# Products of w3 and w_out ahead of block 4's convolution, which moves between second products; w2's first casts on POOL

## The chip, the core and the metric

The kernel runs on one core of one Trainium2 chip. A core has five engines with an instruction queue each: PE (matrix products), DVE and ACT (element-wise work, the only two that take results out of PSUM here), POOL (element-wise work in SBUF, and a queue that issues DMAs) and SP (a queue that only issues DMAs). Sixteen DMA engines move the data of all queues. The metric is the device time of one execution in microseconds (us); less is better.

## What is computed

A light-weight convolution along the sequence, then a multiplicative feed-forward part without any non-linearity:

```python
def _attn_ref(x, weight):                 # x (8, 3904, 192), weight (8, 7)
    w = softmax(weight, axis=-1)          # in the reference written out
    x_pad = zeros(6 rows) + x             # along the sequence
    out[b, s, h, :] = sum_k w[h, k] * x_pad[b, s + k, h, :]   # 8 heads of 24 columns
def _moe_ref(x, w1, w2, w3, w_out):       # x (31232, 192), d_ff 1024
    a = x @ w1
    b = x @ w2
    h = a * b @ w3
    return h @ w_out                      # (31232, 192) fp32
```

Since nothing non-linear stands between w3 and w_out, the kernel forms W = w3 @ w_out once (1024 x 192) and computes (a * b) @ W.

## The kernel before, in words

The 31232 tokens are two halves of 15616 (index r = 0, 1), which lie on partitions 0 to 63 and 64 to 127. Along a half, tokens are cut twice. For the convolution they are *windows* of 58 tokens (64 rows with the 6 of overlap), and windows are grouped in *blocks* (SIZES: 10, 8, 10, 8, then six of 36, then 20). For the products they are *rounds* of 512 tokens, 31 in all, handled in groups of 4.

- `conv(b, h0, nh, evict)` (L273) convolves nh heads of block b: PE multiplies the window's rows (`xb`) with a band matrix (`Aband`), into a pair of PSUM banks (there are four pairs, taken in turn); the engines in `evict` copy the result to `convo` (L290).
- `store(b)` writes `convo` to a DRAM buffer `rows` from SP's queue (L311, L317). `transposes(R)` reads `rows` back, transposed, into `xT` (L346), three DMAs for a round, also on SP's queue. `send(last)` issues the transposes of all rounds that are stored. The blocks 0 to 3 don't go this way: PE transposes them itself (`pe_transpose`, L326).
- `first_product(R)` makes a and b of a round for eight column tiles (L373); ACT copies a to SBUF (L379), and DVE multiplies it with b (L380) into `abT`.
- `second_product(R, r)` multiplies `abT` with `W_sb` (L399); ACT copies the result (L404), and a DMA writes it to the output (L411), in the first group of rounds from POOL's queue, later from SP's.
- `w3_product(jt)` makes an eighth of W (L435) from `w3T` and `wo_b`; ACT copies it to `W_sb` (L437).

`load_w3` casts w3 to bf16 into DRAM by two DMAs of POOL's queue (L425) and reads it back transposed by 16 DMAs of SP's queue (L428); the order is first columns 0 to 511 of all eight row tiles, then 512 to 1023. A tiny copy on POOL (`pace`, L472) waits for one of these transposes and so holds back what stands behind it on POOL's queue: the loads of blocks 4 and 5 (L112). The weights w1 and w2 are needed on both halves of the partitions. Their first quarter of columns comes in fp32 (`wfirst`) and is cast four times (`cast_w(i, r)`, L447), the other quarters come through casting DMAs (L162) and are copied to the upper half (L352).

The order on each queue is that of the program, since the schedule is written out by hand. It runs: weights of the convolution (`warm` keeps PE busy meanwhile, L190); block 0; first_product(0) to (3) with blocks 1 to 3 between their tiles; then block 4's convolution in three slots, heads 0 to 2, 3 to 5, 6 and 7, with three, three and two of the w3 products behind them; then for each group of rounds the first products (from group 1 on), and eight second products with the next block's convolution in the same three slots behind the second, fourth and sixth of them. A block's `store` is called behind its last slot.

Of the kernel before, what the change touches and what calls it, by code (L numbers as in the profile page):

```python
# [16 lines left out]
def kernel(  # L17
# [10 lines left out]
    nc = tc.nc  # L28
# [4 lines left out]
    DFF = moe_w1.shape[1]  # L33
    JT = DFF // 128
# [6 lines left out]
    GROUP = 4  # L41
    RING = GROUP * CH
    Q = 64
# [7 lines left out]
    NB = len(SIZES)  # L51
# [4 lines left out]
    def tok(i):  # L56
        return (i // WB) * S + (i % WB) * ST
# [29 lines left out]
    def halves_of(b):  # L87
        n = SIZES[b] // 2
        return [(FIRST[b], 2 * n)] if 2 * n <= MAXN else [(FIRST[b], n), (FIRST[b] + n, n)]
# [8 lines left out]
    def load_x(b, parts=(0, 1)):  # L98
        tiles = xb_of.setdefault(b, [])
        zeros_of = zero_rows.setdefault(b, [])  # L100
        for i0, n in [v for e, v in enumerate(halves_of(b)) if e in parts]:
            xb = work.tile([128, n, D], BF16, tag="xb", bufs=5, name="xb")
            w = 0
            while w < n:
                i = i0 + w
                m = min(n - w, WB - i % WB)
                at_end = i + m == NWIN
                if at_end:
                    m -= 1
                if m:  # L110
                    for r in range(NS):
                        nc.gpsimd.dma_start(out=xb[Q * r:Q * r + Q, w:w + m, :],  # L112
                                            in_=x_spans(r, i, m))
                if i % WB == 0:
                    zeros_of += [(xb, 0, w), (xb, 1, w)]
                w += m
                if at_end:
                    nc.gpsimd.memset(xb[Q:128, w, :], 0.0)
                    t = tok(NWIN - 1) - PAD
                    nc.gpsimd.dma_start(out=xb[0:Q, w, :], in_=x_rows[t:t + Q, :])  # L120
                    nc.gpsimd.dma_start(out=xb[Q:Q + PAD + LAST, w, :],
                                        in_=x_rows[TS + t:TS + t + PAD + LAST, :])
                    w += 1
            if len(halves_of(b)) == 1:
                tiles += [(xb, 0), (xb, SIZES[b] // 2)]
            else:
                tiles.append((xb, 0))
# [7 lines left out]
    wfirst = work.tile([Q, 2, NP, DFF // 4], FP32, tag="abT", bufs=GROUP, name="wfirst")  # L135
    pace = const.tile([1, 2], BF16)
# [15 lines left out]
    WC = (0, DFF // 4, DFF // 2, DFF * 3 // 4, DFF)  # L152
    wd = [const.tile([128, NP, DFF], BF16, name=f"wd{i}", tag=f"wd{i}") for i in range(2)]
# [5 lines left out]
    def load_w(part):  # L159
        cs = slice(WC[part], WC[part + 1])  # L160
        for i in range(2):
            nc.gpsimd.dma_start(out=wd[i][0:Q, :, cs], in_=w_rows[i][:, :, cs])  # L162
# [5 lines left out]
    for p0 in (0, Q):  # L168
        nc.gpsimd.affine_select(
            out=diag[p0:p0 + Q], in_=ones[p0:p0 + Q].to_broadcast([Q, Q + PAD]),  # L170
# [3 lines left out]
    for r in range(NS):  # L174
        nc.gpsimd.dma_start(out=xb0[Q * r + PAD:Q * r + Q, 0, :],
                            in_=x_rows[r * TS:r * TS + ST, :])
    load_w(1)
    load_w(2)
    load_x(1)
    load_w(3)  # L180
    load_x(2)
# [3 lines left out]
    def warm(n, t=None):  # L185
        p = None
        if t is None:
            p, t = banks()
        for j in range(n):
            nc.tensor.matmul(t[:, j % 2, :], zeros[:, 0:128], zeros, start=True, stop=True)  # L190
        if p is not None:
            drained(p)

    warm(4)

    wmax = const.tile([1, H], FP32)
    wsum = const.tile([1, H], FP32)
# [4 lines left out]
        out=wall, in0=wall, in1=wmax.unsqueeze(2).to_broadcast([1, H, K]), op=ALU.subtract)  # L202
# [6 lines left out]
        out=wrow, in0=wall, in1=wsum.unsqueeze(2).to_broadcast([1, H, K]), op=ALU.mult)  # L209
# [20 lines left out]
    def band(g, e, f):  # L230
        c = slot([128, K, Q], BF16, "cprod")
        nc.vector.tensor_tensor(
            out=c, in0=taps, in1=wsb[:, g, e].unsqueeze(2).to_broadcast([128, K, Q]),
            op=ALU.mult)
        p, bps = banks()
        for v, lhsT in enumerate((ident, swapped)):
            for k in range(K):
                nc.tensor.matmul(bps[:, 0, v * Q:v * Q + Q], lhsT, c[:, k, :],
                                 start=(k == 0), stop=(k == K - 1))
        f(out=Aband[:, g, e].rearrange("p v s -> p (v s)"), in_=bps[:, 0, 0:2 * Q])  # L240
        drained(p)
# [15 lines left out]
    def conv(b, h0, nh, evict=None):  # L257
        n = SIZES[b] // 2
        if h0 == 0:
            convo_of[b] = work.tile([128, n, NP, NS, Q], BF16, tag="convo", bufs=2, name="convo")  # L260
        convo = convo_of[b]
        p, cps = banks()
        wd = nh * G

        def view(ps, r):
            return cps[ps, r, 0:n * wd].rearrange("p (w g) -> p w g", g=wd)

        for j in range(nh):
            h = h0 + j
            for c in range(2):  # L270
                xb, w0 = xb_of[b][c]
                for r in range(NS):
                    nc.tensor.matmul(  # L273
                        view(slice(Q * c, Q * c + Q), r)[:, :, j * G:(j + 1) * G],
                        band_of(h, r),
                        xb[Q * r:Q * r + Q, w0:w0 + n, h * G:(h + 1) * G],
                        start=True, stop=True)
        src = cps[:, :, 0:n * wd].rearrange("p r (w g) -> p r w g", g=wd)
        o, moves = 0, []
        for k, c0, m in segments(h0 * G, wd):  # L280
            moves.append((convo[:, :, k, :, c0:c0 + m].rearrange("p w r g -> p r w g"),
                          src[:, :, :, o:o + m]))
            o += m
        if h0 + nh == H:
            del xb_of[b]
        if evict == ():
            return p, moves
        for e, (dst, part) in enumerate(moves):
            f = evict or [nc.scalar.copy]
            f[e % len(f)](out=dst, in_=part)  # L290
        drained(p)
# [128 lines left out]
    w3T = const.tile([128, JT, DFF], BF16)  # L420
# [11 lines left out]
    def w3_product(jt):  # L432
        p, wps = banks()
        for gt in range(JT):
            nc.tensor.matmul(wps[:, 0, 0:D], w3T[:, gt, jt * 128:(jt + 1) * 128],  # L435
                             wo_b[:, gt, :], start=(gt == 0), stop=(gt == JT - 1))
        nc.scalar.copy(out=W_sb[:, jt, :], in_=wps[:, 0, 0:D])  # L437
        drained(p)


    V, A, P = nc.vector.tensor_copy, nc.scalar.copy, nc.gpsimd.tensor_copy
# [1 line left out]
    def move(f, pair):  # L443
        f(out=pair[0], in_=pair[1])  # L444

    def cast_w(i, r, f):
        f(out=wd[i][Q * r:Q * r + Q, :, 0:WC[1]], in_=wfirst[:, i])  # L447

    cast_w(0, 0, A)
    band(0, 0, A)  # L450
    band(0, 1, A)
    band(1, 0, A)
    band(1, 1, V)
    cast_w(0, 1, A)
    cast_w(1, 1, V)
    cast_w(1, 0, A)
    warm(1)
    for h, f in ((0, V), (2, A), (4, V), (6, A)):
        p, moves = conv(0, h, 2, ())
# [9 lines left out]
            copy_w(part, i, f)  # L469
    load_w3()  # L470
    nc.gpsimd.dma_start(out=wo_b, in_=wor)
    P(out=pace, in_=w3T[0:1, JT // 2 - 1, DFF - 2:DFF])  # L472
    load_x(4)
    load_x(5)

# [6 lines left out]
    def send(last):  # L482
        while sent[0] <= min(last, NR - 1) and min((sent[0] + 1) * CH, TS) <= stored[0]:
            transposes(sent[0])
            sent[0] += 1
# [13 lines left out]
    def zero(b):  # L499
        for xb, r, w in zero_rows.pop(b, []):  # L500
            nc.gpsimd.memset(xb[Q * r:Q * r + PAD, w, :], 0.0)  # L501

    def conv_heads(b, heads):
        for h in heads:
            conv(b, h, 1, (V,))
        if heads[-1] == H - 1:
            store(b)

    slots = (range(0, 3), range(3, 6), range(6, H))
    zero(4)  # L510
    for i, heads in enumerate(slots):
        conv_heads(4, heads)
        for jt in range(3 * i, min(3 * i + 3, JT)):
            w3_product(jt)

    groups = [list(range(R, min(R + GROUP, NR))) for R in range(0, NR, GROUP)]
    assert groups[-1][-1] == NR - 1
    for p, rounds in enumerate(groups):
        b = PROLOGUE_BLOCKS + p
        order = rounds[-1:] + rounds[:-1] if rounds[-1] == NR - 1 else rounds  # L520
        for j, R in enumerate(order if p else ()):
            first_product(R)
            send(R + GROUP)
            if j < 2 and b < NB:
                P(out=pace, in_=abT_of[R][0:1, JT - 1, 1, 0:2])  # L525
                load_x(b, (j,))
        if b < NB:
            zero(b)
        if p == 0:
            send(2 * GROUP - 1)  # L530
        for i, (R, r) in enumerate((R, r) for R in rounds for r in range(NS)):
            second_product(R, r, R == NR - 1 and r == 1, nc.sync if p else nc.gpsimd)
            if i in (1, 3, 5) and b < NB:
                conv_heads(b, slots[i // 2])
    assert sent[0] == NR


# [28 lines left out]
```

## Time and profile before

| | us |
|---|---|
| median of 3 runs | 526.74 (526.51 to 527.09) |
| the profiled execution | 528.84 |
| its span | 527.1 |
| PE busy | 515.7 |
| DVE busy | 362.4 |
| ACT busy | 323.0 |
| POOL busy | 53.9 |

The profile is of one execution. PE, DVE, ACT and POOL are listed with their instructions; SPq is SP's queue of DMA issues, whose lengths are the time of issuing and not of the transfer. "out<-in" names the tiles, "x64" counts merged instructions, and brackets give the idle time of the engine ahead of them with what ended it. The granted PE clock of the core is 1.00.

### The profile page before, as it was taken

The numbers are of one execution on the slowest core, as the hardware profiler recorded it, in microseconds if no ns is written. First come the engines' busy times: TensorE is split into PE (matmuls) and PEld (weight loads), VectorE is DVE, ScalarE is ACT, GpSimd is POOL, SyncE is SP. The second block draws the span as 40 slices with busy tenths as digits, with TensorE's granted clock in tenths as the row PEclk, the third lists the DMA queues.
The fourth block names the chain that finished last, engine by engine and source line by source line (L and its number), as shares of the span: only waits on it lengthen the run. The fifth ranks groups of instructions, "written<-read, shape, count | busy, mean of one in ns | idle before, by whom it ended". The sixth has DMA issues, their size and how long they took to land.

```text
span 527.1 us, 12790 instructions
## 1 busy us (share of the span) xinstructions
PE 515.7 (98%) x5463; PEld 344.6 (65%) x5463; DVE 362.4 (69%) x351; ACT 323.0 (61%) x409; POOL 53.9 (10%) x91
## 2 busy tenths in 40 slices
PE   7999799999999999999999999999999999999997
PEld 4555479655796557955579555895558945599567
DVE  6777855599655996569964699637994289921880
ACT  5888532677526775367743677437774377744762
POOL 8304102112000110001200020000300000000000
PEclk9999999999999999999999999999999999999999
DMA  9997999999648882478834798357643632024004
GB/s 134 229 119 102 180 139 215 191 174 137 111 136 191 113 118 72 140 181 118 111 91 131 170 119 109 91 145 170 90 67 95 169 93 41 17 91 150 2 1 150
DMA packets 133381, 64.59 MB, mean 123 GB/s; under 512 B 90234, under 2 KB 132620, under 8 KB 133260
## 3 DMA queue, kind: packets, MB, share of 16 engines
q1 hardware_dynamic: 94378, 44.10, 38.4%
q0 software_dynamic: 38800, 19.58, 29.6%
q8 instruction: 42, 0.69, 0.6%
q14 instruction: 15, 0.12, 0.1%
q10 hardware_dynamic: 146, 0.10, 0.1%
HBM read 33.25 MB, written 36.52 MB: 132 GB/s over the span
## 4 chain that ended last, share of the span: by engine, by line
PE 85%; DMA 7%; SPq 3%; POOL 2%; DVE 1%; issue 1%; ACT 0%; POOLq 0%; ACTq 0%; DVEq 0%
PE pairs L373 52%; PE pairs L399 30%; DMA xb<-in_x_dram 3%; SPq L428 3%; PE pairs L273 2%; DMA w3rows<-in_moe_w_dram 2%; DMA xT<-rows 1%; POOL xb L112 1%; DVE convo L290 1%; DMA w3T<-w3rows 1%; POOL wd L352 1%; PE pairs L435 0%; POOL wd L162 0%; POOL xb L165 0%; DVE abT L380 0%
## 5 line engine op out<-in xcount | busy, mean ns | idle before, releaser
L380 DVE TENSOR_TENSOR abT<-asb,pairs 128x1024 bf16<-128x1024 bf16 (+1 forms) x248 | 298.5, 1204 | 79.8 <-ACT asb L379 42.6
L373 PE MATMUL pairs<-xT,wd 64*128 64x512 bf16 (+1 forms) x2976 | 320.2, 373 | 1.6 <-DMA xT<-rows 0.6
L379 ACT CAST asb<-pairs 128x1024 bf16<-128x1024 f32 (+1 forms) x248 | 247.6, 998 | 69.2 <-PE pairs L373 68.6
L373 PEld LDWEIGHTS <-wd 64*128 64x128 bf16 x2976 | 165.4, 94 | 150.5 <-issue 3.8
L399 PE MATMUL pairs<-W_sb,abT 128*128 128x192 bf16 x1952 | 165.6, 246 | 0.0
L399 PEld LDWEIGHTS <-abT 128*128 128x128 bf16 x1952 | 159.8, 98 | 8.7 <-issue 8.7
L404 ACT COPY osb<-pairs 128x384 f32<-128x384 f32 x122 | 58.2, 477 | 116.7 <-PE pairs L399 116.7
L290 DVE CAST convo<-pairs 128x864 bf16<-128x864 f32 (+5 forms) x70 | 53.7, 825 | 66.6 <-PE pairs L273 61.3
L112 POOL DMA_DIRECT2D xb<-in_x_dram x40 | 31.0, 791 | 10.1 <-PE pairs L373 6.2
L525 POOL COPY pace<-abT 1x2 bf16<-1x2 bf16 x10 | 1.7, 174 | 241.4 <-DVE abT L380 241.4
L273 PE MATMUL pairs<-xb,Aband 64*64 64x432 bf16 (+3 forms) x352 | 17.4, 294 | 3.3 <-POOL xb L501 2.7
L273 PEld LDWEIGHTS <-Aband 64*64 64x64 bf16 x352 | 7.1, 105 | 10.9 <-issue 9.7
L411 POOL DMA_DIRECT2D out_dram<-osb x8 | 6.1, 758 | 27.8 <-ACT osb L404 27.8
L437 ACT CAST W_sb<-pairs 128x192 bf16<-128x192 f32 x8 | 2.5, 318 | 9.8 <-PE pairs L435 9.8
L404 DVE COPY osb<-pairs 128x192 f32<-128x192 f32 x1 | 0.4, 357 | 11.1 <-PE pairs L399 11.1
L435 PE MATMUL pairs<-wo_b,w3T 128*128 128x192 bf16 x64 | 6.4, 246 | 0.3
L435 PEld LDWEIGHTS <-w3T 128*128 128x128 bf16 x64 | 5.2, 97 | 2.0 <-issue 2.0
L290 ACT CAST convo<-pairs 128x512 bf16<-128x512 f32 (+3 forms) x12 | 5.5, 508 | 0.0
L326 PE MATMUL pairs<-identw,convo 128*128 128x128 bf16 x54 | 4.2, 219 | 1.0 <-DVE convo L444 0.9
L326 PEld LDWEIGHTS <-convo 128*128 128x128 bf16 x54 | 3.2, 97 | 2.8 <-issue 1.5
L190 PE MATMUL pairs<-zeros 128*128 128x512 bf16 x7 | 3.4, 602 | 1.3 <-DVE zeros L145 1.3
L162 POOL DMA_DIRECT2D wd<-in_moe_w_dram x6 | 3.8, 640 | 0.0
(51 smaller groups left out, 39.8 us busy)
## 6 DMA issues: line engine op xcount, KB each, us to landing
out_dram<-osb SPq DMA_DIRECT2D x52, 384.0 KB
xb<-in_x_dram POOLq DMA_DIRECT2D x18, 432.0 KB, 8.4
rows<-convo SPq DMA_DIRECT2D x9, 648.0 KB
out_dram<-osb POOLq DMA_DIRECT2D x8, 384.0 KB, 6.0
w3rows<-in_moe_w_dram POOLq DMA_DIRECT2D x2, 1024.0 KB, 12.4
xb<-in_x_dram POOLq DMA_DIRECT2D x6, 240.0 KB, 7.1
xT<-rows SPq DMA_TRANSPOSE x81
rows<-convo SPq DMA_DIRECT2D x9, 135.0 KB
```

Source lines behind the costliest of these rows:

```text
L112: nc.gpsimd.dma_start(out=xb[Q * r:Q * r + Q, w:w + m, :], in_=x_spans(r, i, m))
L273: nc.tensor.matmul(view(slice(Q * c, Q * c + Q), r)[:, :, j * G:(j + 1) * G], band_of(h, r), xb[Q * r:Q * r + Q, w0:w0 + n, h * G:(h + 1) ...
L290: f[e % len(f)](out=dst, in_=part)
L326: nc.tensor.transpose(out=tps[:, w, :], in_=convo[:, w, k].rearrange("p r g -> p (r g)"), identity=ident)
L373: nc.tensor.matmul(p[:, r, 0:N], wd[i][rs, k, ft * 128:(ft + 1) * 128], xT[k][rs, r0:r0 + N], start=(k == 0), stop=(k == NP - 1))
L379: nc.scalar.copy(out=asb[:, :, 0:N], in_=pa[:, :, 0:N])
L380: nc.vector.tensor_tensor(out=ab[:, ft, :, 0:N], in0=asb[:, :, 0:N], in1=pb[:, :, 0:N], op=ALU.mult)
L399: nc.tensor.matmul(ops[:, (g - g0) * D:(g - g0) * D + D], ab[:, jt, r, g * 128:(g + 1) * 128], W_sb[:, jt, :], start=(jt == 0), stop=(jt = ...
L404: f(out=osb[:, g0:g0 + per, :].rearrange("p g d -> p (g d)"), in_=ops[:, 0:per * D])
L411: queue.dma_start(out=out[t0:t0 + ng * 128, :].rearrange("(g p) d -> p g d", p=128), in_=osb)
L428: nc.sync.dma_start_transpose(out=w3T[:, gt, j:j + CH], in_=w3rows[j:j + CH, gt * 128:(gt + 1) * 128])
L435: nc.tensor.matmul(wps[:, 0, 0:D], w3T[:, gt, jt * 128:(jt + 1) * 128], wo_b[:, gt, :], start=(gt == 0), stop=(gt == JT - 1))
```

## The change

The eight w3 products stand directly behind first_product(3). Heads 0 to 2 of block 4 follow them; heads 3 to 5 stand behind the first second product, heads 6 and 7 (with the store) behind the second. Block 4's evictions alternate between DVE and ACT, head by head. In the first group of rounds block 5's slots stand behind the fourth, sixth and seventh second product in place of the second, fourth and sixth, and the transposes of rounds 4 to 7 are issued behind block 4's store as before. Both first casts of w2 are done by POOL, behind the loads of the second and third quarter of w1 and w2 and ahead of block 1's loads; those of w1 both by ACT, ahead of the bands. One more warm matmul runs at the start. `pace` waits for the transpose of row tile 1 of w3's second half of columns in place of that of row tile 3.

```diff
+    def cast_w(i, r, f):
+        f(out=wd[i][Q * r:Q * r + Q, :, 0:WC[1]], in_=wfirst[:, i])
+
     load_w(1)
     load_w(2)
+    cast_w(1, 0, nc.gpsimd.tensor_copy)
+    cast_w(1, 1, nc.gpsimd.tensor_copy)
     load_x(1)
     load_w(3)
     load_x(2)
...
-    warm(4)
+    warm(5)
...
     cast_w(0, 0, A)
+    cast_w(0, 1, A)
     band(0, 0, A)
     band(0, 1, A)
     band(1, 0, A)
     band(1, 1, V)
-    cast_w(0, 1, A)
-    cast_w(1, 1, V)
-    cast_w(1, 0, A)
     warm(1)
...
-    P(out=pace, in_=w3T[0:1, JT // 2 - 1, DFF - 2:DFF])
+    P(out=pace, in_=w3T[0:1, 1, DFF - 2:DFF])
...
-    def conv_heads(b, heads):
-        for h in heads:
-            conv(b, h, 1, (V,))
+    def conv_heads(b, heads, f=(nc.vector.tensor_copy,)):
+        for j, h in enumerate(heads):
+            conv(b, h, 1, (f[j % len(f)],))
         if heads[-1] == H - 1:
             store(b)
 
     slots = (range(0, 3), range(3, 6), range(6, H))
     zero(4)
-    for i, heads in enumerate(slots):
-        conv_heads(4, heads)
-        for jt in range(3 * i, min(3 * i + 3, JT)):
-            w3_product(jt)
+    for jt in range(JT):
+        w3_product(jt)
+    conv_heads(4, slots[0], (V, A))
...
         if b < NB:
             zero(b)
+        at = {1: [(b, slots[0])], 3: [(b, slots[1])], 5: [(b, slots[2])]}
         if p == 0:
-            send(2 * GROUP - 1)
+            at = {0: [(4, slots[1], (V, A))], 1: [(4, slots[2], (V, A))],
+                  3: at[1], 5: at[3], 6: at[5]}
         for i, (R, r) in enumerate((R, r) for R in rounds for r in range(NS)):
             second_product(R, r, R == NR - 1 and r == 1, nc.sync if p else nc.gpsimd)
-            if i in (1, 3, 5) and b < NB:
-                conv_heads(b, slots[i // 2])
+            for c in at.get(i, ()) if b < NB else ():
+                conv_heads(*c)
+            if p == 0 and i == 1:
+                send(2 * GROUP - 1)
```

More of the change, by code (lines that the diff above doesn't have):

```diff
@@ L444, in move @@
         f(out=pair[0], in_=pair[1])
-    def cast_w(i, r, f):
-        f(out=wd[i][Q * r:Q * r + Q, :, 0:WC[1]], in_=wfirst[:, i])
     cast_w(0, 0, A)
+    cast_w(0, 1, A)
     band(0, 0, A)
```

## The prediction

> **What bounds the kernel now.** I read the page's busy times first, then the chain of waits, then the timelines of PE, DVE, SP and POOL between 44 and 114 us and of all engines in the first 18 us. Columns of the chain: start, length, what; of the timelines: start, length, engine, line, operation, and in brackets the idle time before and who ended it.
>
> ```profile
> span 527.1 us, 12790 instructions
> PE 515.7 (98%) x5463; PEld 344.6 (65%) x5463; DVE 362.4 (69%) x351; ACT 323.0 (61%) x409; POOL 53.9 (10%) x91
> ```
>
> PE is busy for 98%, so only its idle times can be won, some 11 us. The chain shows the largest below 100 us.
>
> ```profile
> 71.55 1.43 PE pairs L435 x16
> ...
> 78.26 0.67 PE pairs L273 x12
> ...
> 90.93 6.44 DMA xT<-rows
> ...
> 97.41 41.18 PE pairs L373 x380
> 138.59 5.39 PE pairs L399 x64
> ```
>
> From 97.41 on PE runs from product to product with no wait on the chain: whatever the change does ahead of that moment, the end moves by as much as the start of first_product(4) moves. That start is set by a DMA, xT<-rows, and not by PE. PE's own list shows how close the two were:
>
> ```profile
> 47.34 13.28 PE L373 MATMUL pairs<-xT,wd 64*128 64x512 bf16 x120
> ...
> 63.44 0.34 PE L273 MATMUL pairs<-xb,Aband 64*64 64x432 bf16 x1 [2.52 <-POOL xb L501]
> 63.98 0.70 PE L273 MATMUL pairs<-xb,Aband 64*64 64x432 bf16 x9 [0.20 <-POOL xb L501]
> ...
> 67.46 0.74 PE L273 MATMUL pairs<-xb,Aband 64*64 64x432 bf16 x12 [0.21 <-DVE convo L290]
> ...
> 70.99 0.56 PE L273 MATMUL pairs<-xb,Aband 64*64 64x432 bf16 x8 [0.21 <-DVE convo L290]
> ...
> 96.18 0.60 PE L373 MATMUL pairs<-xT,wd 64*128 64x512 bf16 x4
> 97.41 2.96 PE L373 MATMUL pairs<-xT,wd 64*128 64x512 bf16 x25 [0.62 <-DMA xT<-rows]
> ```
>
> first_product(3) ends at 47.34+13.28=60.62. Then PE idles 2.52+0.20+0.21+0.21=3.14 us inside block 4's convolution, arrives at first_product(4) at 96.18 and waits 0.62 us there. The chain behind xT is this:
>
> ```profile
> 71.42 2.02 DVE L290 CAST convo<-pairs 128x864 bf16<-128x864 f32 x2 [0.48 <-PE pairs L273]
> 73.47 0.34 SPq L317 DMA_DIRECT2D rows<-convo  x1
> ...
> 79.68 2.48 SPq L311 DMA_DIRECT2D rows<-convo  x1
> 82.20 4.17 SPq L317 DMA_DIRECT2D rows<-convo  x2
> 86.55 1.88 SPq L346 DMA_TRANSPOSE xT<-rows  x1
> ```
>
> The last eviction of block 4 ends at 71.42+2.02=73.44; SP then issues the seven copies of store(4) until 86.37 and the transposes of round 4 from 86.55; the third, issued at 90.93, lands at 97.37. From eviction to xT: 97.37-73.44=23.93 us. This chain starts at the **end of the convolution of block 4**, and that is the point the change moves.
>
> **The change part by part.** *Products first.* The 64 matmuls of w3 x w_out now follow first_product(3) at once: 16 took 1.43 us, so 0.089 each and 5.7 us (bounds 5.4, what 64 of L399 take, and 6.8, the stretches they needed among the convolutions). Then come conv heads 0 to 2 (0.67), second_product(0,0) (half of 5.39: 2.69), heads 3 to 5 (0.67), second_product(0,1) (2.69), heads 6 and 7 (0.56): 12.98 us together. Nothing here waits for block 4's loads, which land at 63.09 (below). The eviction of the last head is by ACT; its price isn't in the trace at this size, so I take DVE's 2.02/2=1.0 us.
>
> *The first casts.* In the beginning:
>
> ```profile
> 7.62 1.69 ACT L447 CAST wd<-wfirst 64x768 bf16<-64x768 f32 x2
> ...
> 8.40 0.95 DVE L447 CAST wd<-wfirst 64x768 bf16<-64x768 f32 x1
> 9.38 1.29 DVE L444 CAST convo<-pairs 128x480 bf16<-128x480 f32 x3
> ...
> 8.43 0.82 PE L273 MATMUL pairs<-xb,Aband 64*64 64x120 bf16 x32
> 10.19 1.12 PE L326 MATMUL pairs<-identw,convo 128*128 128x128 bf16 x15 [0.94 <-DVE convo L444]
> ...
> 3.75 0.21 PE L215 MATMUL pairs<-wrow,half 1*128 1x28 bf16 x2 [0.53 <-DVE wrow L208]
> ```
>
> PE's convolution of block 0 begins at 8.43, but DVE evicts from 9.38 only, behind its cast, and ACT is busy with two casts until 7.62+1.69=9.31. Without them both can start near 8.7, as the first heads are done: for DVE 0.65 earlier. I take 0.6 us off the transposes and the start of first_product(0) (at most the 0.94 idle). One w1 cast stays on ACT, moved ahead of the bands; it delays the first band's eviction by some 0.2 us, with three other banks open to PE. The fifth warm matmul lies in the 0.53 us for which PE waits for wrow.
>
> POOL takes both w2 casts between load_w(2) and load_x(1):
>
> ```profile
> 8.31 0.68 POOL L112 DMA_DIRECT2D xb<-in_x_dram  x1 [0.36 <-DMA xb<-in_x_dram]
> ...
> 13.11 3.12 POOL L352 COPY wd<-wd 64x768 bf16<-64x768 bf16 x4
> ...
> 16.83 0.36 PE L273 MATMUL pairs<-xb,Aband 64*64 64x96 bf16 x16
> xb<-in_x_dram POOLq DMA_DIRECT2D x1, 192.0 KB, 5.2
> ```
>
> A POOL copy of this size from bf16 takes 0.78; from fp32 no row exists, so 0.78 to twice that, and I take the lower, nearest row: 1.6 us (to 3.1) for two. Everything behind them on POOL's queue is later by that: both load_x(1), load_w(3), load_x(2) and (3), POOL's copies of parts 2 and 3, both w3 loads, wo_b. Block 1's second load (8.31+5.2=13.5, the last row being its time to landing) comes at 15.1, while conv(1) is due at 16.83-0.6=16.2: covered, by 1.1 us. At the upper price it is late by 0.4 us; POOL's first copy for part 2 (13.11+0.78+3.1=17.0) is late by about as much. So the prologue gives 0.6 us, between 0.95 gained and 0.5 lost.
>
> *The pace.* It waits for the tenth transpose of w3T in place of the twelfth.
>
> ```profile
> 39.85 1.26 SPq L428 DMA_TRANSPOSE w3T<-w3rows  x1
> ...
> 42.46 4.10 DMA w3T<-w3rows
> ...
> 49.98 13.11 DMA xb<-in_x_dram
> ```
>
> That is 42.46-39.85=2.6 us earlier, less the 1.6 us by which w3 is late: block 4's loads start about 1 us earlier (2.6 earlier to 0.5 later). They landed at 49.98+13.11=63.09 and are first needed at 65.7 now: this edit is worth nothing where it stands, hidden by the products.
>
> *The sum.* first_product(3) ends at 60.62-0.6=60.0; plus 12.98 gives 73.0; plus 1.0 the last eviction, **74.0 against 73.44**. PE itself goes on with second_product(1,0) to (3,1) and block 5's convolution, 5.39+0.67+5.39+0.67+2.69+0.56+2.69=18.1, and reaches first_product(4) at 91.0, 5.2 us earlier than its 96.18. It finds no xT. What the chain from eviction to xT takes then decides.
>
> ```profile
> 105.34 6.34 SPq L317 DMA_DIRECT2D rows<-convo  x4
> 113.32 2.06 SPq L346 DMA_TRANSPOSE xT<-rows  x1
> 76.44 0.79 POOL L411 DMA_DIRECT2D out_dram<-osb  x1 [12.51 <-ACT osb L404]
> ...
> 85.12 0.75 POOL L411 DMA_DIRECT2D out_dram<-osb  x1 [1.89 <-ACT osb L404]
> ...
> 94.42 0.75 POOL L411 DMA_DIRECT2D out_dram<-osb  x1 [2.48 <-ACT osb L404]
> ```
>
> Block 5, with as many rows and no output copies beside it, goes from store to first transpose in 113.32-105.34=8.0 us; block 4 needed 86.55-73.47=13.1 us with four output copies (76.44 to 85.12) beside it: some 1.3 us for each. Output copies come 0.8 us behind their second product (the first ended at 71.55+1.43+2.69=75.67, its copy is issued at 76.44), now at 69.8, 73.2, 76.5, 79.2, 82.5, 85.2, 88.6 and 91.8. Six lie where there were six; the one at 73.2 is new beside the start of the store (+1.3), and those of 94.42 and later are gone from the end of the transposes (up to -1.3). I take 23.93 unchanged, between 1.3 less and 1.3 more. [...]
>
> first_product(4) goes on at 74.0+23.93=97.9 in place of 97.4: **+0.5 us**. The profiled execution took 528.84 (span 527.1) and would take 529.3; on the median of 526.74 that is **527.2**. All 5.2 us that PE wins turn into idle time between 91.0 and 97.9.
>
> **The rivals.** *PE comes back slow* (the other side). Idle for 6.9 us, with two pairs of matmuls in between as parts of xT land, PE may lose its pace:
>
> ```profile
> 1.33 1.89 PE L190 MATMUL pairs<-zeros 128*128 128x512 bf16 x4 [1.33 <-DVE zeros L145]
> ...
> 3.89 1.03 PE L190 MATMUL pairs<-zeros 128*128 128x512 bf16 x2
> ...
> 7.86 0.46 PE L190 MATMUL pairs<-zeros 128*128 128x512 bf16 x1
> ```
>
> After the launch, four 512-column matmuls come 0.43 us apart ((1.89-1.03)/2, four against two); in first_product the two row halves run side by side, 13.28/60=0.22 per 512 columns: half pace. Slow lasted at least until 4.92 and at most until about 8 us, 3.6 to 6.7 us from the first matmul, each losing half: 1.8 to 3.3 us. The 2.52 us gap at 63.44 cost nothing (0.34 us for its next matmul), so it decides from a gap above that. Start at 97.9, then +2.5: 526.74+0.5+2.5=**529.7**. Against it: the matmuls in between cut the gap into pieces near 2.5 us. [...]
>
> *The chain shortens.* If the missing late output copies matter more than the new early one, the third transpose lands as w3T's did, 4.10 us from issue in place of 6.44: -2.3+0.5=-1.8, **524.9**. For it: output copies end 5 us earlier. Against: the store in front is no less crowded.
>
> *The change does what it says in full.* xT is there when PE arrives at 91.0: 6.4 us less, **520.3**. It needs a chain of 17 us where even uncrowded parts make 8.0+2.5+4.1=14.6 (store, two issues of 1.26, a landing); with six output copies beside it hardly.
>
> *POOL's casts cost* their upper price and the prologue loses 0.5 where I have a gain of 0.6: +1.1, **528.3**.
>
> **How the numbers follow.** Forecast 0.40; slow PE 0.28; shorter chain 0.20; POOL 0.08; in full 0.04. 0.2% of 526.7 is 1.05 us, about what a measurement of this kernel tells from nothing. The forecast (its terms spread by some 1.1 us about +0.5) gives 0.03 faster, 0.25 same, 0.12 slower; slow PE 0.01 same, 0.27 slower; shorter chain 0.15 faster, 0.05 same; POOL 0.02 same, 0.06 slower; in full 0.04 faster. Sum: faster 0.22, same 0.33, slower 0.45. The likeliest case alone runs from 526.0 to 528.6; with the rivals, leaving a tenth at each end, 524.7 to 530.0.
>
> **What would show it.** The w3 products in one piece of 5.7 us from about 60.0 with no idle; transposes of block 0 from about 9.6; first output copy near 69.8; SP's first copy of store(4) near 74.0 and its first transpose near 87; PE idle, released by xT<-rows, from 91 to about 98. Slow PE shows as L373 matmuls near 1.03-0.43=0.60 us each behind 98 us and ACT waiting twice as long for them. Wrong I am if PE meets a landed xT, if store(4) starts below 73 us, or if PE waits for xb or wd before 25 us.

## The result and the profile after

| | before | after |
|---|---|---|
| first comparison, median | 526.62 us (526.34 to 527.09, 4 runs) | 530.83 us (530.22 to 531.34, 4 runs) |
| its ratio | | 1.0079, 95% interval 1.0061 to 1.0096 |
| second comparison (e1), median | 526.96 us (34 runs) | 529.92 us (11 runs) |
| its ratio | | 1.0045, 95% interval 1.0027 to 1.0064 |
| span of the profiled execution | 527.1 | 528.3 |

By the ratios the changed kernel is slower, by 2.4 us (1.4 to 3.4) in the larger comparison and by 4.2 us in the first (0.6% to 1.0%); the medians of the larger one lie 3.0 us apart. Most of the difference between the two comparisons lies in the executions that they caught, as the mean granted PE clock of each run shows. In e1's comparison the kernel before has 23 runs at 0.999 or 1.000 (median 526.54), ten at 0.996 or 0.997 (528.53) and one at 0.994 (530.51); the changed kernel has three at 0.997 (528.89) and eight at 0.992 or 0.993 (530.08). In the first comparison all four runs of the changed kernel are at 0.993, and none of the four of the kernel before took more than 527.1. Full clock against 0.993 is 3.5 us in e1; why the first comparison gave 0.7 us more than that stays open. The two spans differ by 1.2 us only; why, e5 shows.

The page of the changed kernel has one digit in its clock row that the page of before did not have (third line, 40 equal slices of the span, tenths of full clock):

```profile
span 528.3 us, 12785 instructions
PE 516.0 (98%) x5464; PEld 342.1 (65%) x5464; DVE 359.1 (68%) x347; ACT 325.0 (62%) x411; POOL 55.5 (10%) x93
...
PEclk9999999799999999999999999999999999999999
```

The 7 is the slice from 92 to 106 us. PE's list there (lines of the changed kernel are up to five higher, L378 is first_product, L404 second_product, L440 the w3 products, L278 the convolution):

```profile
59.99 5.45 PE L440 MATMUL pairs<-wo_b,w3T 128*128 128x192 bf16 x64
65.38 0.74 PE L278 MATMUL pairs<-xb,Aband 64*64 64x432 bf16 x12
...
88.05 2.81 PE L404 MATMUL pairs<-W_sb,abT 128*128 128x192 bf16 x32
93.44 0.39 PE L378 MATMUL pairs<-xT,wd 64*128 64x512 bf16 x2 [2.57 <-DMA xT<-rows]
94.85 0.61 PE L378 MATMUL pairs<-xT,wd 64*128 64x512 bf16 x2 [1.02 <-DMA xT<-rows]
96.62 19.57 PE L378 MATMUL pairs<-xT,wd 64*128 64x512 bf16 x162 [1.17 <-DMA xT<-rows]
```

No idle time is left between 59.99 and 90.86, as forecast, and then PE waits three times for parts of xT, 4.8 us in all. The two matmuls between took 0.39 us together at 93.44 and 0.61 us at 94.85. The stretches of the same execution, each with PE's busy time, the granted clock behind the engines' times, then DMA share and GB/s:

```profile
93.00:94.00 1.00, 0.39 (x2) 0.11 (x3) 0.00 (x0) 0.00 (x0) 0.00 (x0) 0.85 1.00 325
94.00:95.00 1.00, 0.15 (x2) 0.10 (x2) 0.00 (x0) 0.00 (x0) 0.00 (x0) 0.50 1.15 418
...
99.00:100.00 1.00, 1.00 (x7) 0.36 (x5) 0.83 (x1) 0.17 (x1) 0.00 (x0) 0.50 0.29 64
100.00:101.00 1.00, 1.00 (x10) 0.53 (x8) 0.03 (x1) 0.85 (x1) 0.00 (x0) 0.74 0.53 118
101.00:102.00 1.00, 1.00 (x13) 0.46 (x11) 1.00 (x1) 0.45 (x1) 0.00 (x0) 1.00 0.58 131
```

The granted clock falls to 0.50 at about 93.7 (a microsecond with mean 0.85 had 0.7 of it at 1.00) and returns at about 100.5; meanwhile PE gets 7 or 8 matmuls a microsecond instead of 13. The chain of waits gives the price:

```profile
91.04 5.54 DMA xT<-rows
...
96.62 43.09 PE pairs L378 x380
139.72 5.39 PE pairs L404 x64
```

Before, the stretch began at 97.41 and lasted 41.18. It begins 0.79 us earlier and lasts 1.91 us longer: 1.12 us later at its end, and that is the difference of the spans but for 0.1 us.

### The profile page after: what moved, and what is told of

The parts are those of the page before. It is cut to its first block, busy times and chain, and to the rows that moved or that the text cites. A ratio compares the mean times of both kernels' runs of the same rounds, so it can differ in the third digit from the quotient of the medians.

```text
span 528.3 us, 12785 instructions
## 1 busy us (share of the span) xinstructions
PE 516.0 (98%) x5464; PEld 342.1 (65%) x5464; DVE 359.1 (68%) x347; ACT 325.0 (62%) x411; POOL 55.5 (10%) x93
## 4 chain that ended last, share of the span: by engine, by line
PE 93%; DMA 2%; DVE 2%; ACT 2%; issue 0%; POOL 0%; SPq 0%; POOLq 0%; ACTq 0%
PE pairs L378 58%; PE pairs L404 31%; PE pairs L278 2%; DVE abT L385 2%; ACT asb L384 1%; DMA xT<-rows 1%; PE pairs L440 1%; DMA xb<-in_x_dram 1%; PE pairs L331 1%; POOL xb L165 0%; DVE convo L449 0%; ACT xT L449 0%; ACT xT L343 0%; POOL diag L169 0%; ACT convo L295 0%
## 5 line engine op out<-in xcount | busy, mean ns | idle before, releaser
L378 PE MATMUL pairs<-xT,wd 64*128 64x512 bf16 (+1 forms) x2976 | 322.5, 374 | 5.8 <-DMA xT<-rows 4.8
L378 PEld LDWEIGHTS <-wd 64*128 64x128 bf16 x2976 | 164.5, 94 | 157.9 <-issue 8.0
L404 PEld LDWEIGHTS <-abT 128*128 128x128 bf16 x1952 | 159.6, 98 | 9.7 <-issue 9.7
L404 PE MATMUL pairs<-W_sb,abT 128*128 128x192 bf16 x1952 | 165.9, 246 | 0.0
L295 DVE CAST convo<-pairs 128x864 bf16<-128x864 f32 (+5 forms) x67 | 50.8, 814 | 67.3 <-PE pairs L278 67.3
L278 PE MATMUL pairs<-xb,Aband 64*64 64x432 bf16 (+3 forms) x352 | 16.6, 294 | 1.0 <-DMA xb<-in_x_dram 1.0
L278 PEld LDWEIGHTS <-Aband 64*64 64x64 bf16 x352 | 6.6, 105 | 7.9 <-issue 6.9
L295 ACT CAST convo<-pairs 128x512 bf16<-128x512 f32 (+4 forms) x15 | 8.1, 584 | 0.3 <-PE pairs L278 0.2
L440 PEld LDWEIGHTS <-w3T 128*128 128x128 bf16 x64 | 5.2, 98 | 0.4 <-issue 0.4
L440 PE MATMUL pairs<-wo_b,w3T 128*128 128x192 bf16 x64 | 5.5, 246 | 0.0
L501 POOL MEMSET xb<- 6x192 bf16 x6 | 1.5, 250 | 21.7 <-DMA xb<-in_x_dram 21.7
```

Of the source, the lines that this page charges most:

```text
L278: nc.tensor.matmul(view(slice(Q * c, Q * c + Q), r)[:, :, j * G:(j + 1) * G], band_of(h, r), xb[Q * r:Q * r + Q, w0:w0 + n, h * G:(h + 1) ...
L378: nc.tensor.matmul(p[:, r, 0:N], wd[i][rs, k, ft * 128:(ft + 1) * 128], xT[k][rs, r0:r0 + N], start=(k == 0), stop=(k == NP - 1))
L404: nc.tensor.matmul(ops[:, (g - g0) * D:(g - g0) * D + D], ab[:, jt, r, g * 128:(g + 1) * 128], W_sb[:, jt, :], start=(jt == 0), stop=(jt = ...
```

## The experiments

All edits are against the changed kernel or the kernel before, as said; ratios are to the kernel before, measured beside them.

**e1, the changed kernel again.** No edit.

> The changed kernel once more, against the kernel before in the same rounds. Its trace shows first_product(4) resuming at 96.62 where before it resumed at 97.41 (0.8 us earlier), and PE at a granted clock of 0.50 from about 93.9 to 100.5, which makes the stretch up to the next second product 43.09 long in place of 41.18 (1.9 us more). Theory: these two are all there is, so the ratio is about (526.6+1.1 to 1.5)/526.6, 1.002 to 1.003. Rival: something outside the profiled span costs the rest of the 4.2 us first measured, and the ratio comes out near 1.008 again.

Measured: 529.92 us, ratio 1.0045 (1.0027 to 1.0064), between the two expectations. Its trace resumes at 96.36 and runs 43.59 us to the second product:

```profile
96.36 43.59 PE pairs L378 x380
```

The 34 times of the kernel before go from 525.3 to 530.5, those of this kernel from 528.5 to 530.8: the kernel before varies far more. So its one profile need not stand for its median.

**e5, the kernel before, profiled again.**

> The kernel before, unchanged, one more profile. Its 34 times beside the first four experiments run from 525.3 to 530.5, its one profile has 2.5 us of idle PE ahead of block 4's convolution at clock 1.00 and took 528.8. Theory: the loads of block 4 land at another moment in each execution, and where PE idles long enough ahead of them the clock falls; this trace then has another idle time there than 2.5 us, or a clock below 1.00 near 62 us. Rival: the idle time and the clock are the same as in the first profile, and the spread comes from elsewhere.

Measured: 526.85 us, span 525.1, clock 1.00 throughout these stretches. PE's list and, below it, the chain:

```profile
62.27 1.01 PE L273 MATMUL pairs<-xb,Aband 64*64 64x432 bf16 x10 [1.35 <-POOL xb L501]
...
94.77 9.46 PE L373 MATMUL pairs<-xT,wd 64*128 64x512 bf16 x84
```

```profile
95.42 41.18 PE pairs L373 x380
```

The wait for block 4's load is 1.35 us instead of 2.52, and first_product(4) starts without a wait, its stretch 2.0 us earlier than in the first profile. This execution lies at the median, the first one (528.84) 2.1 us above it. (That the clock falls in some executions of this kernel is in the eleven runs of e1's comparison below 0.998; where it falls, no trace of this kernel shows.) Against e5, e1's trace resumes 0.94 us later and has 2.41 us of slow clock: 3.4 us, and its span is 528.5 against 525.1. The 0.79 us gain against the first profile was a gain against a late execution.

**e2, PE kept busy in the gap** (changed kernel).

```diff
         for j, R in enumerate(order if p else ()):
+            if p == 1 and j == 0:
+                warm(24)
             first_product(R)
```

> The changed kernel with 24 matmuls on zeros in PE's queue ahead of first_product(4), 24 x 0.22 = 5.2 us, so that PE works from about 90.9 to 96.1 while it would wait for xT. Theory (the gap costs by the clock alone): no matmul at 0.50 behind 96 us, first_product(4) still starts near 96.6, its stretch is 41.2 long again, and the time falls by about 1.9 us against the changed kernel, to 0.8 us below the kernel before. Rival (the slow stretch has nothing to do with idleness, for example the DMAs' crowd): 0.50 appears all the same, no gain.

```profile
90.98 5.34 PE L195 MATMUL pairs<-zeros 128*128 128x512 bf16 x24
96.25 0.61 PE L378 MATMUL pairs<-xT,wd 64*128 64x512 bf16 x4
97.21 15.07 PE L378 MATMUL pairs<-xT,wd 64*128 64x512 bf16 x138 [0.35 <-DMA xT<-rows]
```

```profile
97.21 41.19 PE pairs L378 x380
```

Measured: 528.05 us, ratio 1.0015 (0.9997 to 1.0033), 1.9 us below e1. The stretch is back at 41.19 and the clock at 1.00. The mean clock is 0.999 or 1.000 in all twelve runs, where all fifteen of the changed kernel (the first four and e1's) have 0.997 or less. That the slow stretch comes from idleness is shown; nearly the same DMA crowd was there (245 GB/s and a DMA share of 0.86 from 92 to 96 us, 264 and 0.95 in the changed kernel). The expected gain over the kernel before did not come, for two reasons: that kernel starts at 95.4 in e5 and not at 97.4, and here PE restarts at 97.21 and not near 96.6, since the last part of xT lands later in this execution (SP issues the first transpose at 87.47; it was 86.54).

**e4, the order alone** (kernel before; casts, warm matmuls and pace left).

```diff
-    for i, heads in enumerate(slots):
-        conv_heads(4, heads)
-        for jt in range(3 * i, min(3 * i + 3, JT)):
-            w3_product(jt)
+    for jt in range(JT):
+        w3_product(jt)
+    conv_heads(4, slots[0], (V, A))
...
+            for c in at.get(i, ()) if b < NB else ():
+                conv_heads(*c)
+            if p == 0 and i == 1:
+                send(2 * GROUP - 1)
```

> The kernel before with the change's order alone: the eight w3 products first, block 4's heads behind them and between second products, evictions by DVE and ACT; casts, warm matmuls and pace as before. Theory: everything as in the changed kernel but 0.6 us later, first_product(4) resumes near 97.3 after some 5.5 us of idle PE, at clock 0.50: 1.8 to 2.5 us above the kernel before, ratio 1.003 to 1.005. Rival (the losses come from POOL's casts): this order is not slower than before.

```profile
94.41 0.61 PE L373 MATMUL pairs<-xT,wd 64*128 64x512 bf16 x4 [3.01 <-DMA xT<-rows]
96.76 15.47 PE L373 MATMUL pairs<-xT,wd 64*128 64x512 bf16 x118 [1.74 <-DMA xT<-rows]
```

```profile
96.76 43.74 PE pairs L373 x380
```

Measured: 530.28 us, ratio 1.0050 (1.0030 to 1.0069), as much as the whole change, with a mean clock of 0.997 or less in all twelve runs. The order loses this much without POOL's casts.

**e3 and e10, the start alone** (kernel before, with the casts, warm(5) and pace of the change).

```diff
+    cast_w(1, 0, nc.gpsimd.tensor_copy)
+    cast_w(1, 1, nc.gpsimd.tensor_copy)
     load_x(1)
...
-    warm(4)
+    warm(5)
...
     cast_w(0, 0, A)
+    cast_w(0, 1, A)
...
-    P(out=pace, in_=w3T[0:1, JT // 2 - 1, DFF - 2:DFF])
+    P(out=pace, in_=w3T[0:1, 1, DFF - 2:DFF])
```

> The kernel before with the change's start alone: first casts of w2 by POOL, those of w1 by ACT, the fifth warm matmul, and pace on the tenth transpose. Block 4's convolution and the w3 products stand as they stood before. Theory (the end moves with the last eviction of block 4): first_product(3) ends at 60.0, block 4's last load is there by about 59, so the 2.5 us of waiting for it go, the last eviction ends near 70.2 in place of 73.4, xT lands near 93.5 to 94, PE arrives near 92.5 and waits about a microsecond at full clock: 3 to 4 us less than before, ratio 0.993 to 0.994. Rival (the output copies and not the eviction set xT): xT lands as late as 96 to 97, and less than 1 us is gained.

> The kernel of e3_start_only, one more profile: its profiled execution (530.5 us) was the slowest of its 13, median 525.75, with clock 0.50 from about 61 to 69 us behind a wait of 2.2 us for block 4's load. Theory (the fall of the clock in a gap of 2 to 3 us happens in some executions): time within 1 us of 525.75, clock 1.00 throughout, the wait for block 4's load under 2 us. Rival: clock 0.50 again.

Measured: 525.75 us, ratio 0.9975 (0.9954 to 0.9996): 1.3 us gained and not 3 to 4. Its profiled execution was the slowest of the 13 (530.54). PE's list, and two stretches:

```profile
62.36 1.76 PE L278 MATMUL pairs<-xb,Aband 64*64 64x432 bf16 x10 [2.22 <-POOL xb L501]
64.05 4.02 PE L440 MATMUL pairs<-wo_b,w3T 128*128 128x192 bf16 x24
```

```profile
62.00:63.00 1.00, 0.63 (x5) 0.37 (x9) 0.00 (x0) 0.00 (x0) 0.50 (x2) 0.53 1.61 194
...
68.00:69.00 1.00, 1.00 (x13) 0.37 (x12) 0.37 (x1) 0.32 (x1) 0.00 (x0) 0.55 1.60 191
```

Here the clock fell at about 62.1, in a gap of 2.2 us, shorter than the 2.52 us that cost nothing in the first profile of before, and came back at about 68.9. The three w3 products took 4.02 us instead of 2.64. The second profile (e10, 526.47 us) has the load in time and no such gap; from PE, SP and the chain:

```profile
59.84 1.25 PE L278 MATMUL pairs<-xb,Aband 64*64 64x432 bf16 x12
```

```profile
70.58 6.53 SPq L322 DMA_DIRECT2D rows<-convo  x4
```

```profile
94.17 41.19 PE pairs L378 x380
```

The store starts 1.48 us earlier than e5's (72.06) and the stretch 1.25 us earlier (95.42). That fits an end that follows the last eviction of block 4, but PE's own arrival moved as far (93.30 against 94.77), so these runs don't tell the two apart; the changed kernel and e6 do. The expectation failed in its baseline, again the late first profile.

**e7, six output copies left out** (changed kernel; rounds 0 to 2).

```diff
-        if not last:
+        if not last and R > 2:
             queue.dma_start(
```

> The changed kernel without the six output copies of rounds 0 to 2 (their rows of the output are left out); everything else in place. Theory (each output copy beside them costs the store and the transposes 1.2 to 1.3 us): store in 8 us and three transposes in 6.6 us from the last eviction at 73.7, xT by 88.5 to 89.5, so no wait at 90.9, clock 1.00, 7 us less than the changed kernel, ratio to before 0.990 to 0.993. Rival (SP's issuing sets the chain): first transpose near 86.5 and xT near 96.5 as with the copies.

SP's queue, then PE:

```profile
73.69 6.54 SPq L322 DMA_DIRECT2D rows<-convo  x4
80.28 1.32 SPq L316 DMA_DIRECT2D rows<-convo  x1
81.64 1.63 SPq L322 DMA_DIRECT2D rows<-convo  x2
83.45 16.34 SPq L351 DMA_TRANSPOSE xT<-rows  x12
```

```profile
87.98 2.81 PE L404 MATMUL pairs<-W_sb,abT 128*128 128x192 bf16 x32
90.73 13.55 PE L378 MATMUL pairs<-xT,wd 64*128 64x512 bf16 x124
```

Measured: 522.71 us, ratio 0.9930 (0.9905 to 0.9956), clock 1.00 in the trace, no wait at 90.7. The copies do stretch the chain past PE's arrival. But store to first transpose takes 83.45-73.69=9.8 us without them, and 86.54-73.76=12.8 us with them in the changed kernel (87.25-73.66=13.6 in e1), so 3.0 to 3.8 us for the four to five copies that lie there: 0.6 to 1.0 each, less than the 1.3 I charged.

**e11, one output copy left out** (changed kernel; round 0, second half).

```diff
-        if not last:
+        if not last and (R, r) != (0, 1):
```

> The changed kernel without the one output copy of round 0, second half, which it issues at 73.1 just ahead of the store (those rows of the output are left out). The prediction charged it 1.3 us. Theory: first transpose 1 to 1.3 us earlier than 86.5, xT near 95.4, slow clock as before: 1 us less than the changed kernel. Rival (a copy ahead of the store is nearly done when the store starts): no change in the first transpose within 0.4 us.

```profile
74.38 5.94 SPq L322 DMA_DIRECT2D rows<-convo  x4
...
86.43 18.82 SPq L351 DMA_TRANSPOSE xT<-rows  x12
```

```profile
96.54 43.16 PE pairs L378 x380
```

The store began 0.6 us later here and the first transpose is as early: 12.05 us against 12.78. That is not yet 0.7 us for the copy: with all copies in place the same stretch took 12.78 and 13.59 us in two executions of the changed kernel, and 13.08 and 11.24 in two of the kernel before (e5's first transpose is issued at 83.30), so one execution doesn't give the price of one copy. The first transpose itself comes 0.1 us earlier, which is the rival's side. The time was 527.05 us, ratio 1.0014 (0.9994 to 1.0035), 2.9 us below e1, though the profiled execution (530.10, slow clock) is as slow as e1's. The mean clocks sort the ten times: three at 0.993 (529.1 to 530.1 us), four at 0.996 or 0.997 (527.0 to 528.0) and three at 1.000 (525.0 to 526.9). Why the clock falls less often and for less time than in the changed kernel isn't shown.

**e8, the gap of the kernel before filled** (kernel before).

```diff
     zero(4)
+    warm(13)
```

> The kernel before with 13 matmuls on zeros (2.8 us) in PE's queue between first_product(3) and block 4's convolution, where it waits for the load. Theory (in part of its executions the kernel before loses clock in that wait): the spread of times narrows, none near 528 to 530.5, median the same or up to 1 us lower. Rival: the same spread of 5 us and the same median.

```profile
60.11 2.98 PE L190 MATMUL pairs<-zeros 128*128 128x512 bf16 x13
63.02 1.13 PE L273 MATMUL pairs<-xb,Aband 64*64 64x432 bf16 x12
```

```profile
62.58 0.25 POOL L501 MEMSET xb<- 6x192 bf16 x1 [3.87 <-DMA xb<-in_x_dram]
63.15 0.25 POOL L501 MEMSET xb<- 6x192 bf16 x1 [0.32 <-DMA xb<-in_x_dram]
```

```profile
96.54 41.19 PE pairs L373 x380
```

Measured: 527.78 us, ratio 1.0018 (1.0008 to 1.0028), times from 527.2 to 528.7, all at a mean clock of 0.999 or 1.000; of the 17 runs of the kernel before beside them three are at 0.996 or 0.997. The spread narrowed as expected, but three times are above 528 and the median rose by 0.9 us. In this trace the filler hardly holds anything up: its 13 matmuls end at 63.1, and the second of block 4's loads lands at 63.15, as POOL's memsets behind the loads show. Where the load is in time for a start at 62.27, as in e5, the filler would overshoot by some 0.8 us (an estimate from these two traces). That the lowest time rose from 525.83 to 527.16 fits this, but no trace shows it.

**e6 and e9, block 4 early.** The products cover the load with three of them and are then spread among the heads; e6 has the start of the change, e9 that of the kernel before.

```diff
-    for jt in range(JT):
-        w3_product(jt)
-    conv_heads(4, slots[0], (V, A))
+    for heads, jts in ((None, range(0, 3)), (slots[0], range(3, 5)),
+                       (slots[1], range(5, 7)), (slots[2], range(7, JT))):
+        if heads:
+            conv_heads(4, heads, (V, A))
+        for jt in jts:
+            w3_product(jt)
+    send(2 * GROUP - 1)
```

> The changed kernel with block 4's heads earlier: three w3 products, heads 0 to 2, two products, heads 3 to 5, two products, heads 6 and 7 with store and transposes, the last product; then the second products with block 5's heads as in the kernel before. The three products cover block 4's loads. Theory (xT follows the last eviction): last eviction near 67.5 in place of 73.7, third transpose landed by 91 at the latest, so PE meets it without waiting at 90.9 and at clock 1.00: against the changed kernel 5.7 us of waiting and 1.9 us of slow clock less, some 7 us, ratio to the kernel before 0.990 to 0.993. Rival (the output copies or block 5's loads set xT's landing, whenever the store starts): xT lands near 94 to 96 again and at most 2 us are gained.

> The early order of e6_early with the start and the pace of the kernel before: casts on ACT and DVE, four warm matmuls, pace on the twelfth transpose. Theory (the order decides; the start gives its 0.6 us and the earlier pace keeps block 4's loads covered): first_product(3) ends at 60.6 in place of 60.0, block 4's last load at 62 to 63.5 is up to 1 us later than the three products cover, no wait for xT: 0.6 to 1.6 us above e6_early, ratio to before 0.995 to 0.998. Rival (the start gives nothing by itself): the same as e6_early, 0.9945.

SP and PE of e6:

```profile
68.45 6.01 SPq L322 DMA_DIRECT2D rows<-convo  x4
...
80.71 18.46 SPq L351 DMA_TRANSPOSE xT<-rows  x12
```

```profile
86.10 5.46 PE L404 MATMUL pairs<-W_sb,abT 128*128 128x192 bf16 x64
91.49 12.69 PE L378 MATMUL pairs<-xT,wd 64*128 64x512 bf16 x116
```

Measured: e6 523.90 us, ratio 0.9945 (0.9926 to 0.9964), span 521.6, clock 1.00, no idle PE at first_product(4). It beats both kernels: the kernel before by 3.0 us, the changed one (529.92 in e1) by 6.0 us; I had expected a little more, a ratio of 0.990 to 0.993. e9:

```profile
91.93 12.41 PE L373 MATMUL pairs<-xT,wd 64*128 64x512 bf16 x112
```

524.18 us, 0.9949 (0.9929 to 0.9968). The start is worth 0.4 us at the end here (91.93 in place of 91.49) and nothing that the times tell apart; the 0.6 to 1.6 us that I expected were too much, since in e9's execution block 4's loads came in time all the same.

## Why the prediction was wrong

Its mechanism holds: the end moves with the restart of first_product(4), plus the slow clock behind it; that restart waits for xT, and xT follows the last eviction of block 4; PE's earlier arrival is lost in a wait. The points of the working, beside the changed kernel's queues:

```profile
7.30 1.70 POOL L178 CAST wd<-wfirst 64x768 bf16<-64x768 f32 x2
...
42.05 0.17 POOL L472 COPY pace<-w3T 1x2 bf16<-1x2 bf16 x1 [22.66 <-DMA w3T<-w3rows]
...
58.82 0.25 POOL L501 MEMSET xb<- 6x192 bf16 x1 [4.56 <-DMA xb<-in_x_dram]
```

```profile
10.63 5.66 PE L378 MATMUL pairs<-xT,wd 64*128 64x512 bf16 x48
...
72.85 0.88 ACT L295 CAST convo<-pairs 128x864 bf16<-128x864 f32 x1
...
86.54 2.16 SPq L351 DMA_TRANSPOSE xT<-rows  x1
```

- *The start.* 0.6 us forecast; first_product(0) begins at 10.63 instead of 11.24. POOL's casts take 0.85 each (0.78 taken). Right.
- *The pace.* 1 us earlier forecast; it passes at 42.05 instead of 46.62, and block 4's loads are there at 58.8 instead of 63.1. More than forecast in this pair of traces; in all traces together it passes at 42.05 to 45.39 with the new start and at 43.45 to 47.14 with the old one. Hidden, as forecast.
- *Last eviction* 74.0 forecast, 72.85+0.88=73.73 measured; PE's arrival 91.0, measured 90.86. Right.
- *The chain* 23.93 us taken, 96.62-73.73=22.9 measured. The price of 1.3 us for an output copy came from block 5's store, whose four DMAs take 8.0 us; block 4's seven take 9.8 with no copy beside them (e7), so less was the copies' doing: 0.6 to 1.0 each by e7. The chain came out 1.0 us shorter than taken, inside the bounds given; whether by the late copies that went, no run shows, and e11 doesn't tell what the early one cost.
- **The step that failed: "the matmuls in between cut the gap into pieces near 2.5 us"**, by which slow PE had 0.28 and the likeliest case full clock. The pieces came out no longer than said (2.57, 1.02 and 1.17 us), and the clock fell all the same. It was 0.50 in all four traces in which PE waits this way (the changed kernel, e1, e4, e11), in e11 with no piece above 1.97 us, and the mean clock was 0.997 or less in all fifteen runs of the changed kernel. e2 removes the loss. So pieces shorter than the 2.52 us gap that had cost nothing are no protection; in e3 the clock fell in a single gap of 2.2 us. The price, 1.8 to 3.3 us, was right: 1.9, 2.4, 2.6 and 2.0 us from the stretches 43.09, 43.59, 43.74 and 43.16.
- **A second step: "on the median of 526.74 that is 527.2".** The +0.5 was worked out against an execution 2.1 us slower than the median, and the surplus lay just where the change acts, in the wait for block 4's loads. A changed kernel that no longer depends on those loads doesn't inherit their good days. From e5's start at 95.4, my own 97.9 would have meant +2.5 us even at full clock, and the measured restarts of 96.4 and 96.6 mean about 1 us besides the slow clock.

The rival of slow PE gave 529.7; 529.92 and 530.83 were measured. Its sign came (matmuls of 0.63 us each behind 96.6, for the 0.60 forecast), but that its sum lies so near is partly luck: PE restarted 1.3 us earlier than its 97.9, and e5 starts 2.0 us earlier than the 97.41 from which it was reckoned.

## What to carry to other kernels

Filling a wait with work from behind it gains nothing if what ends the next wait starts later for it: move first what feeds the longest chain of DMAs (block 4's eviction in e6), and fill with the rest. PE's idle time can cost more than its length (behind PE's 4.8 us of waiting in the changed kernel another 1.9 us went at a clock of 0.50), so a wait that is "only moved" is to be priced with the clock behind it. And where the profiled execution lies above the median, look for what varies before carrying a difference from one to the other.

## What the runs showed of the hardware

The half clock (a granted clock of 0.50) lasted 6.8 to 6.9 us in each of the five traces that have it: 93.70 to 100.52 in the changed kernel, 94.44 to 101.28 in e1, 62.06 to 68.90 in e3 (edges from the means of the one-microsecond stretches), 95.1 to 102.0 in e4 and 93.8 to 100.6 in e11 (from stretches of four). It began 1.9 to 3.7 us after PE's last dense work (60.14 in e3, 90.86 in the changed kernel, 90.76 in e1), and a pair of matmuls in the gap did not hold it up (93.44 in the changed kernel, 0.26 us ahead of the fall). A gap of 2.2 us brought it on in e3 and one of 2.5 us did not in the first profile of before, so the length alone doesn't decide. In other executions the half clock was probably shorter: the five traces have mean clocks of 0.993 or 0.994, while 0.996 or 0.997 over 526 us would be some 3 to 4 us at half clock (an estimate; none of those runs has a trace).

In e3 PE was idle for 0.3 us behind the fall (62.06 to 62.36) and busy throughout from then on, and the clock came back only at 68.90: 6.5 us of work ran at 0.50. What sets the moments of the fall and of the return, no run here shows.
